# Block products for the last three token pairs of the first two QKV column groups, with the router's columns riding on them

## The chip, the cores and the metric

One core of one Trainium2 chip runs the whole layer in one program. The metric is the device time of one execution in microseconds, the median of several; lower is better.

## The reference

```python
xn = layernorm(x)                                  # [2048, 512]
qkv = xn @ wqkv                                    # 32 heads of 16, split into q, k, v
logits = q . k at 8 positions back, step 2         # sliding window, dilation 2
A = softmax(logits * 16**-0.5) @ v  ->  @ wo
top2 of  x @ w_gate (8 experts);  gates = softmax of the two
B = sum over the two experts  gate * silu(x @ w1[e]) @ w2[e]      # F = 1792
out = x + A(xn) + B(xn)
```

Both halves get the normalised input. Results are float32.

## The kernel before

**Numbers.** Matmuls take float16. A float32 operand is split into a rounded high part and a float16 remainder, and a product is three passes: high by high, low by high, high by low. So a QKV tile (128 tokens, one of four column groups `cg` of 3 x 128 columns, four blocks `kb` of the inner dimension) is twelve matmuls: passes `h` and `l` in line 384, pass `w` in line 382 (`q_pass`).

**Front.** Tokens are in 16 tiles `j`. Each is loaded, normalised (`ln_bn` to `ln_nm`), split (`x_hi`, `x_lo`), stored for the experts (`x_store`) and turned so that the inner dimension lies on partitions (`x_turn`, a DMA transpose on SyncE's queue, task `tn_j`; the first four tiles by TensorE). Column groups 0 and 1 go tile by tile (`seq`, line 1109). The router's eight columns stand beside group 0's weights (`gate_part`, lines 290 to 296): 400 columns in passes `h` and `l`.

**Block products.** Groups 2 and 3 are done for pairs of token tiles `p_` with Strassen's scheme (Winograd's form): seven products `m1` to `m7` of half the inner dimension instead of eight, each six matmuls of 384 columns (`product`, line 482). They need sums of feature blocks on VectorE for four tiles at a time (`f_join` L440, `s_sums` L447 to L450, `s_hi` on ScalarE L461, `s_lo` L464) and sums of weight blocks (`w_sum` L419, `u_hi` L430, `u_lo` L433). Results are put together by `take`: ScalarE copies `x11`, `x12`, `x22`, `xu`, `x21` (L506), VectorE adds `y11`, `y12`, `y22` (L508, L500). Products `m1`, `m6`, `m7`, `m4` add up in one PSUM bank, and between them ScalarE copies the bank out: `m6` waits for `x11`, `m7` for `x12`, `m4` for `xu`.

**Router.** When the last tile's gate columns are out of PSUM (`q_gl`, L407), VectorE runs `r_top` (L536 to L567), TensorE counts (`r_count`, L571), VectorE runs `r_rank` (L579 to L616) and three steps `r_hot` (L632 to L638), TensorE makes the token lists (`r_list`, L645, 16 matmuls twice), VectorE casts them (L648). GpSimd then gathers tokens (L852), SyncE turns them (L859), and TensorE begins with the first expert's `up` (L923). GpSimd's first list of constants is `c_lists`; the attention mask is `c_mask` (L233).

**Order.** A planner (`Plan.solve`) lists tasks with engine, cost, dependencies and due times, and fixes for each engine one order; every engine, and SyncE's DMA queue, then works in that order and waits where an operand is late. Attention's VectorE work (L781 on) fills the rest up to the end.

Of the kernel before, what the change touches and what calls it, by code (L numbers as in the profile page):

```python
# [17 lines left out]
P = 128  # L18
S = 2048
# [30 lines left out]
NPAIR = 10  # L50
# [6 lines left out]
NP0 = 0  # L57
# [5 lines left out]
class Plan:  # L63
    def __init__(self):
        self.tasks = {}

    def add(self, name, eng, dur, fn, deps=(), prio=0.0, svc=0.0, early=0.0, begun=(), lead=None, post=0.6):
        assert name not in self.tasks, name
        self.tasks[name] = (eng, dur, fn, [d for d in deps if d is not None], prio, svc, early,
                            [d for d in begun if d is not None], lead, post)  # L70

    def solve(self, start):
# [74 lines left out]
        self.begin, self.end, self.order, self.late = begin, end, order, late  # L147
# [19 lines left out]
def layer_kernel(ctx: ExitStack, tc, x, wqkv, wo, wg, w1, w2, out):  # L167
# [11 lines left out]
    qd = dp.tile([NCH, 3, 16 + S, H2], F32, name="qd")  # L179
# [18 lines left out]
    low_e = cp.tile([P, E, E], F32, name="low_e")  # L198
# [15 lines left out]
    def c_lists():  # L214
# [15 lines left out]
        nc.gpsimd.iota(it, pattern=[[1, MAXT]], channel_multiplier=0, **io)  # L230

# [13 lines left out]
    glog = rtp.tile([P, NJ, 2 * E], F32, name="glog")  # L245
# [44 lines left out]
    def gate_part():  # L290
        if 0 not in wq:
            wq[0] = frp.tile([P, KB, 784], F16, name="wq_0", tag="wq")
# [3 lines left out]
        nc.gpsimd.tensor_tensor(t[:, :, 392:400], gs, t[:, :, 384:392], op=ALU.subtract)  # L296
# [6 lines left out]
    def ln_bn(j):  # L303
        st = fre.tile([P, 6], F32, name=f"bs_{j}", tag="bs")
        v.bn_stats(st, xt_(j))
        mv = fre.tile([P, 2], F32, name=f"mv_{j}", tag="mv", bufs=4)
        v.bn_aggr(mv, st)
        L[j] = dict(mv=mv)

    def ln_rs(j):  # L310
        rs = fre.tile([P, 1], F32, name=f"rs_{j}", tag="rs", bufs=4)
        if j < N32:
            nc.scalar.activation(rs, L[j]["mv"][:, 1:2], AF.Sqrt, bias=eps, scale=1.0)
        else:
# [1236 lines left out]
```

## Time and profile before

| | |
|---|---|
| median of 3 runs | 759.71 us (759.58 to 759.80) |
| the profiled execution | 759.23 us |
| its span, first to last instruction | 757.5 us |
| TensorE busy | 750.4 us, 99% |
| VectorE busy | 665.1 us, 88% |
| ScalarE busy | 400.3 us, 53% |
| GpSimd busy | 110.3 us, 15% |

Times within the profile count from the first instruction; the profiled execution is 1.73 us longer than its span and 0.48 us shorter than the median. A busy share is an average over stages; a wait in TensorE's order counts fully only if it ends last.

### The profile page before, as it was taken

The page shows a single profiled execution, that of the slowest core. Times are in us where ns is not written, and L with a number is a line of the kernel's source. Part 1 is how long each engine was busy: PE and PEld are TensorE (multiplying, and loading weights), DVE is VectorE, ACT ScalarE, POOL GpSimd, SP SyncE. Part 2 cuts the span into 40 slices and gives each one's busy share as a digit, 9 for nine tenths or more (in the row PEclk, how much of TensorE's full clock was granted, in tenths as well). Part 3 has the DMA queues.
Part 4 walks back from the last instruction along what each step waited for, and adds up shares of the span by engine and source line. Part 5 has one row for each costly group of instructions (what it writes and reads, how often), then busy time and mean ns, then how long its engine had stood idle before and what let it go on. Part 6 is the DMA issues. An engine that isn't in the chain of part 4 may idle for free.

```text
span 757.5 us, 12466 instructions
## 1 busy us (share of the span) xinstructions
PE 750.4 (99%) x4950; PEld 415.7 (55%) x4950; DVE 665.1 (88%) x632; ACT 400.3 (53%) x596; POOL 110.3 (15%) x107
## 2 busy tenths in 40 slices
PE   8999999999999999999999999999999999999997
PEld 5555665555555555555555555555555555555544
DVE  8897999999999899989999989999999899737365
ACT  6875356555467445754654564465447554753300
POOL 2010036040001300300040004002100000007271
PEclk9999999999999999999999999999999999999999
DMA  8999899685359547994683599457526943986485
GB/s 279 225 267 333 277 213 316 246 230 180 119 179 218 184 158 218 217 227 121 223 250 127 193 245 260 132 179 211 204 85 170 247 129 112 219 325 203 138 255 192
DMA packets 167378, 157.26 MB, mean 208 GB/s; under 512 B 81505, under 2 KB 135137, under 8 KB 167059
## 3 DMA queue, kind: packets, MB, share of 16 engines
q1 hardware_dynamic: 161571, 139.52, 64.4%
q0 software_dynamic: 5216, 16.88, 7.6%
q8 instruction: 40, 0.66, 0.4%
q14 instruction: 23, 0.19, 0.1%
q10 hardware_dynamic: 528, 0.02, 0.0%
HBM read 108.12 MB, written 29.56 MB: 182 GB/s over the span
## 4 chain that ended last, share of the span: by engine, by line
PE 98%; SPq 1%; DMA 1%; DVE 0%; issue 0%; ACT 0%
PE pu L924 13%; PE pu L923 13%; PE pu L925 13%; PE y L956 10%; PE y L955 10%; PE y L954 10%; PE pw L1093 5%; PE pq L384 5%; PE pm_a L492 4%; PE yt L965 3%; PE pq L382 3%; PE pm_d L492 2%; PE yt L966 2%; PE yt L974 2%; PE yt L972 2%; PE yt L973 2%
## 5 line engine op out<-in xcount | busy, mean ns | idle before, releaser
L924 PE MATMUL pu<-xgt,w 128*128 128x64 f16 (+8 forms) x616 | 184.7, 321 | 0.0
L923 PE MATMUL pu<-xgt,w 128*128 128x64 f16 (+8 forms) x616 | 184.5, 321 | 0.0
L925 PE MATMUL pu<-xgt,w 128*128 128x64 f16 (+8 forms) x616 | 180.4, 321 | 0.0
L931 ACT ACTIVATE hs<-pu 128x64 f32<-128x64 f32 (+8 forms) x154 | 69.8, 481 | 183.8 <-PE pu L925 182.6
L898 DVE SCALAR_TENSOR_TENSOR w<-s,w 128x2048 f16<-128x2048 f32 (+1 forms) x57 | 128.3, 2250 | 18.6 <-ACT w L889 18.3
L889 ACT ACTIVATE w<-s 128x2048 f16<-128x2048 f32 (+1 forms) x57 | 107.3, 1883 | 60.2 <-PE yt L966 28.2
L956 PE MATMUL y<-w,hh 128*128 128x512 f16 x336 | 127.5, 379 | 0.0
L954 PE MATMUL y<-w,hh 128*128 128x512 f16 x336 | 127.5, 379 | 0.0
L955 PE MATMUL y<-w,hh 128*128 128x512 f16 x336 | 127.5, 379 | 0.0
L852 POOL DMA_INDIRECT xg<-xr,lis x35 | 65.6, 1874 | 419.3 <-DMA xgt<-xg 359.5
L941 DVE SCALAR_TENSOR_TENSOR hh<-hs,hh 128x550 f16<-128x550 f32 (+7 forms) x112 | 76.7, 687 | 26.2 <-ACT hh L937 26.1
L925 PEld LDWEIGHTS <-w 128*128 128x128 f16 x616 | 58.9, 97 | 48.4
L923 PEld LDWEIGHTS <-w 128*128 128x128 f16 x616 | 59.3, 98 | 40.9
L924 PEld LDWEIGHTS <-w 128*128 128x128 f16 x616 | 59.0, 98 | 40.8
L937 ACT ACTIVATE hh<-hs 128x550 f16<-128x550 f32 (+7 forms) x112 | 70.5, 630 | 3.4
L808 DVE TENSOR_TENSOR pv<-vt,at 128x4096 f32<-128x4096 f32 x16 | 70.8, 4422 | 0.3
L781 DVE TENSOR_TENSOR pq<-kt,qt 128x4096 f32<-128x4096 f32 x16 | 70.7, 4421 | 0.2
L785 DVE TENSOR_REDUCE at<-pq 128x256 f32<-128x4096 f32 x16 | 70.6, 4414 | 0.0
L1076 POOL DMA_INDIRECT yg<-yd,yrow x32 | 36.0, 1125 | 173.9 <-DMA s<-in_B_w 145.9
L814 DVE TENSOR_TENSOR pv<-pv 128x2048 f32<-128x2048 f32 (+1 forms) x32 | 56.1, 1754 | 0.2
L956 PEld LDWEIGHTS <-hh 128*128 128x128 f16 x336 | 32.9, 98 | 39.6
L955 PEld LDWEIGHTS <-hh 128*128 128x128 f16 x336 | 32.9, 98 | 34.1
(207 smaller groups left out, 1019.4 us busy)
## 6 DMA issues: line engine op xcount, KB each, us to landing
s<-in_B_w SPq DMA_DIRECT2D x112, 512.0 KB
kt<-qd SPq DMA_DIRECT2D x8, 960.0 KB
vt<-qd SPq DMA_DIRECT2D x8, 960.0 KB
qd<-qe SPq DMA_DIRECT2D x8, 768.0 KB
qd<-qp SPq DMA_DIRECT2D x8, 768.0 KB
yd<-ys SPq DMA_DIRECT2D x24, 256.0 KB
xr<-xh SPq DMA_DIRECT2D x16, 256.0 KB
qt<-qd SPq DMA_DIRECT2D x8, 512.0 KB
```

What stands on the lines that cost most here:

```text
L781: v.tensor_tensor(A["pr"].rearrange("p (j w d) -> p j w d", w=WIN, d=H2), a_win(A["k", c], hf, False), qb.to_broadcast([P, 8, WIN, H2]), o ...
L785: v.tensor_reduce(A["at", c][:, 8 * hf:8 * hf + 8].rearrange("p j w h -> p (j w h)"), A["pr"].rearrange("p (n d) -> p n d", d=16), axis=AX ...
L808: v.tensor_tensor(A["pr"].rearrange("p (j w h d) -> p j w h d", w=WIN, h=NH, d=16), a_win(A["v", c], hf, True), ab.to_broadcast([P, 8, WIN ...
L889: nc.scalar.activation(w[:, 0, c_], stg[k][:, c_], AF.Copy, scale=SW)
L898: v.scalar_tensor_tensor(w[:, 1, c_], stg[k][:, c_], SW, w[:, 0, c_], op0=ALU.mult, op1=ALU.subtract)
L923: nc.tensor.matmul(ps, a_[:, 0, kb, fs], xh, start=kb == 0, stop=False)
L924: nc.tensor.matmul(ps, a_[:, 0, kb, fs], xl, start=False, stop=False)
L925: nc.tensor.matmul(ps, a_[:, 1, kb, fs], xh, start=False, stop=kb == KB - 1)
L941: v.scalar_tensor_tensor(hh[:, 1, c_], hsd[key, f][:, c_], SH, hh[:, 0, c_], op0=ALU.mult, op1=ALU.subtract)
L954: nc.tensor.matmul(y_, hi, b_[:, 0, :], start=st, stop=False)
L955: nc.tensor.matmul(y_, hi, b_[:, 1, :], start=False, stop=False)
L956: nc.tensor.matmul(y_, lo, b_[:, 0, :], start=False, stop=sp)
```

## The change

Groups 0 and 1 (`s_` = 0) now go tile by tile only for the first ten tiles (pairs 0 to 4), and by block products for pairs 5, 6 and 7. All eight pairs of groups 2 and 3 (`s_` = 1) stay block products, in the order 4, 5, 6, 7, 0, 1, 2, 3. There are eleven block instances `i_` (`INST`), and every task name ends in `i_`: `m4_2` is product `m4` of pair 7 of groups 0 and 1.

The router's columns are 392 wide in all three passes (before: 400 in two). On the block pairs they ride on `m1`, `m7`, `m2` and `m4`, and ScalarE takes them out of three banks (`take_gate`); the last to come is that of `m4_2`. New are four weight sums and four split units for groups 0 and 1. The feature blocks come in the order 2, 3, 0, 1. The loads of the weights of groups 2 and 3 come after the units of groups 0 and 1. QKV results are stored per token pair (16 stores) in another layout of the scratch. The router's code is shortened by a few VectorE instructions (two memsets, three copies, a comparison with two sums, a subtraction). Normalisation takes two tiles' square roots in one instruction. The mask is set up on GpSimd right after the constants. The last instance keeps its bank `a` in another PSUM buffer. The warm-up matmuls are 11 of 512 columns instead of 44 of 128.

The diff, cut:

```diff
-NPAIR = 10
-NP0 = 0
+NP1 = 5
+SECOND = (4, 5, 6, 7, 0, 1, 2, 3)
+INST = [(0, p_) for p_ in range(NP1, NS)] + [(1, p_) for p_ in SECOND]
+NA, NI = NS - NP1, len(INST)
+BO = list(dict.fromkeys(p_ // 2 for _, p_ in INST))
...
+        nc.gpsimd.tensor_copy(tok16, tokf)
+        nc.gpsimd.memset(scan, 0.0)
+        nc.gpsimd.memset(mask, 0.0)
...
     def warm_up(n):
         for _ in range(n):
-            for q_ in range(KB):
-                nc.tensor.matmul(pwarm[:, q_ * P:(q_ + 1) * P], warm[:, 0:P], warm[:, q_ * P:(q_ + 1) * P], start=True, stop=True)
+            nc.tensor.matmul(pwarm, warm[:, 0:P], warm, start=True, stop=True)
...
+    def right_of(s_, n, a, k):
+        if s_:
+            return unit[1, n][:, a, k]
+        if n[0] == "b":
+            kh, cg = int(n[1]) - 1, int(n[2]) - 1
+            return wq[cg][:, 2 * kh + k, 392 * a:392 * a + (384 if cg else 392)]
+        return unit[0, n][:, a, k, 0:392 if n in ("t3", "t4") else 384]
...
+    def take_gate(i_, m):
+        p_ = INST[i_][1]
+        dst, bank = dict(m1=(glog[:, 2 * p_, :], "a"), m2=(gadd[:, p_ - NP1, :], "c"), m4=(glog[:, 2 * p_ + 1, :], "a"))[m]
+        nc.scalar.activation(dst, MB[i_, bank][:, 384:392], AF.Copy, scale=-1.0 / (SW * SX))
...
     seq = [(0, 0), (0, 1), (1, 0), (1, 1)]
-    seq += [(cg, j) for j in range(2, NPAIR) for cg in (0, 1)]
-    seq += [(0, j) for j in range(NPAIR, NJ)] + [(1, j) for j in range(NPAIR, NJ)]
-    seq += [(cg, j) for j in range(2 * NP0) for cg in (2, 3)]
+    seq += [(cg, j) for j in range(2, 2 * NP1) for cg in (0, 1)]
...
-    add("zero", "DVE", 0.6, lambda: v.memset(mask, 0.0), deps=["nm_5"])
-    add("c_mask", "POOL", 1.8, c_mask, deps=["zero"])
+    add("c_mask", "POOL", 1.8, c_mask, deps=["c_lists"])
...
-        add(f"lwq{cg + 2}", "SP", 2.6, B(load_wq, cg + 2, range(KB), nc.sync), deps=[f"wl{cg}_{kb}" for kb in range(KB)],
-            svc=2.7, begun=["tn_8"])
+        add(f"lwq{cg + 2}", "SP", 2.6, B(load_wq, cg + 2, range(KB), nc.sync), deps=[f"wl{cg}_{kb}" for kb in range(KB)] +
+            ([["ul0_t3", "ul0_t4"], ["ul0_t1", "ul0_t2", "t3_0", "t4_0"]][cg] if NA else []), svc=2.7, begun=["tn_8"])
...
         after = dict(m1=[], m2=[], m6=["x11"], m7=["x12"], m5=[], m4=["xu"], m3=["x22"])
+        if s_ == 0:
+            after["m7"] = ["x12", "gm1"]
...
-    gl = [f"gl_{j}" for j in range(NJ)]
-    add("r_top", "DVE", 6.2, r_top, deps=gl + ["c_lists"], prio=-10.0)
+    gl = [f"gl_{j}" for j in range(2 * NP1)] + [f"g{m}_{i}" for i in range(NA) for m in ("m1", "m2", "m4")]
+    add("r_top", "DVE", 5.3, r_top, deps=gl + ["c_lists"], prio=-10.0)
```

Three places show how instructions move.

**VectorE before the first results are added.** Before, the second feature block (`f_1`) and the weight sums stand ahead of the router's first row (L536), and no result of a block product is due yet:

```order
L440 TENSOR_TENSOR f_1_819<-xnT_103 128x2048
L447 TENSOR_TENSOR f_1_819<-f_1_819 128x4x128
L448 TENSOR_TENSOR f_1_819<-f_1_819 128x4x128
L449 TENSOR_TENSOR f_1_819<-f_1_819 128x4x128
L450 TENSOR_TENSOR f_1_819<-f_1_819 128x4x128
L419 TENSOR_TENSOR wqs_3_624<-wqs_3_624,wqs_2_778 128x768
L419 TENSOR_TENSOR wqs_3_624<-wqs_3_624 128x768
L433 SCALAR_TENSOR_TENSOR wx_b11_860<-wqs_2_778,wx_b11_860 128x768
L433 SCALAR_TENSOR_TENSOR wx_t1_895<-wqs_3_624,wx_t1_895 128x768
L419 TENSOR_TENSOR wqs_2_778<-wqs_3_624,wqs_2_778 128x768
L464 TENSOR_TENSOR sw_1_878<-f_1_819,sw_1_878 128x2x512 x2
L536 TENSOR_TENSOR lg_973<-glog_104 128x128
```

Now (`qp_0_5` is the output tile of pair 5, the first instance; `pm_0_c` its bank `c`):

```order
L495 TENSOR_TENSOR sw_2_760<-f_2_702,sw_2_760 128x2x512 x2
L462 SCALAR_TENSOR_TENSOR u0_t4_721<-wqs_0_160,u0_t4_721 128x2x384
L471 TENSOR_TENSOR f_3_804<-xnT_104 128x2048
L478 TENSOR_TENSOR f_3_804<-f_3_804 128x4x128
L479 TENSOR_TENSOR f_3_804<-f_3_804 128x4x128
L480 TENSOR_TENSOR f_3_804<-f_3_804 128x4x128
L481 TENSOR_TENSOR f_3_804<-f_3_804 128x4x128
L545 TENSOR_TENSOR qp_0_5_780<-qp_0_5_780 128x6x64
L554 SCALAR_TENSOR_TENSOR qp_0_5_780<-pm_0_d_797,qp_0_5_780 128x6x64
L554 SCALAR_TENSOR_TENSOR qp_0_5_780<-pm_0_c_762,qp_0_5_780 128x6x64
L495 TENSOR_TENSOR sw_3_850<-f_3_804,sw_3_850 128x2x512 x2
```

The second block's join and sums now stand ahead of the three sums of the first instance; the last of these, `y11_0`, frees the bank that TensorE's product `m2_2` writes.

**TensorE around the router's count.** Before, the count (`pr`) stands between the last tile of group 1 and the first block product:

```order
L382 MATMUL pq_1_15_1053<-wq_1_268,xnT_103 128x384
L571 LDWEIGHTS tri_73
L571 MATMUL pr_1068<-rsum_1006,tri_73 128x8
L572 LDWEIGHTS tri_73
L572 MATMUL pr_1068<-rsum_1006,tri_73 128x8
L492 LDWEIGHTS xnT_103
L492 MATMUL pm_0_a_1071<-wx_b11_860,xnT_103 128x384
```

Now it stands between two products of the fifth instance (pair 5 of groups 2 and 3), `m1_4` and `m6_4`, which share bank `a`:

```order
L531 MATMUL pm_4_a_1074<-wx_b11_899,xnT_104 128x384
L619 LDWEIGHTS tri_73
L619 MATMUL pr_1084<-rsum_1051,tri_73 128x8
L620 LDWEIGHTS tri_73
L620 MATMUL pr_1084<-rsum_1051,tri_73 128x8
L531 LDWEIGHTS sw_2_760
L531 MATMUL pm_4_a_1074<-wq_3_967,sw_2_760 128x384
```

`m1_5` and `m6_5` stand side by side in the same way. From the end of `m4_2`, whose gate columns come last, to the second half of the lists, TensorE's order holds 20 products and the first half of the lists.

**GpSimd at the start.** Before, the gate columns (L294 to L296) follow the constants, and the mask comes after them:

```order
L230 IOTA it_84 128x48
L294 TENSOR_SCALAR wq_0_211<-gs_186 128x4x8
L295 TENSOR_SCALAR gs_186<-gs_186 128x32
L296 TENSOR_TENSOR wq_0_211<-gs_186,wq_0_211 128x4x8
L233 AFFINE_SELECT mask_85<-mask_85 128x512
```

Now:

```order
L252 IOTA it_85 128x48
L253 CAST tok16_81<-tokf_77 128x16
L254 MEMSET scan_82 128x576
L255 MEMSET mask_86 128x512
L258 AFFINE_SELECT mask_86<-mask_86 128x512
L319 TENSOR_SCALAR wq_0_190<-gs_162 128x4x8
L320 TENSOR_SCALAR gs_162<-gs_162 128x32
L321 TENSOR_TENSOR wq_0_190<-gs_162,wq_0_190 128x4x8
```

The gate columns, which the first QKV matmul reads, moved behind two memsets and the mask.

## Rows read from the trace of the kernel before

**Rows 1.** The page of the profile, part 1: busy us, share of the span and instructions of each engine.
```profile
PE 750.4 (99%) x4950; PEld 415.7 (55%) x4950; DVE 665.1 (88%) x632; ACT 400.3 (53%) x596; POOL 110.3 (15%) x107
```

**Rows 2.** The chain of work that ended last, its shares of the span by engine (page, part 4).
```profile
PE 98%; SPq 1%; DMA 1%; DVE 0%; issue 0%; ACT 0%
```

**Rows 3.** Busy time by stretch of the span: stretch and its length, then busy us (and instructions) of PE, PEld, DVE, ACT, POOL, then granted clock, DMA share, GB/s.
```profile
20.00:30.00 10.00, 10.00 (x63) 5.89 (x62) 9.39 (x21) 9.38 (x24) 0.00 (x0) 1.00 0.95 196
...
50.00:60.00 10.00, 10.00 (x63) 5.90 (x62) 9.52 (x11) 6.29 (x13) 0.00 (x0) 1.00 1.12 244
60.00:70.00 10.00, 10.00 (x63) 5.95 (x62) 6.19 (x20) 4.60 (x11) 0.00 (x0) 1.00 1.04 359
...
90.00:100.00 10.00, 10.00 (x86) 6.25 (x83) 9.90 (x15) 5.29 (x10) 2.12 (x2) 1.00 0.80 249
```

**Rows 4.** The chain that ended last in order of time, 0 to 170 us: start, us, what. L384 and L382 are the passes of an ordinary QKV tile, L492 a block product.
```profile
48.55 1.35 PE pq L384 x8
...
70.32 1.30 PE pq L384 x8
...
88.90 0.98 PE pm_d L492 x6
...
90.27 0.98 PE pm_a L492 x6
```

**Rows 5.** ScalarE in order of time: start, us, engine, line, what, and in brackets the idle time before it and what ended it.
```profile
47.17 1.05 ACT L461 CAST sw<-f 128x1024 f16<-128x1024 f32 x1
50.59 1.25 ACT L402 ACTIVATE qe<-pq 128x384 f32<-128x384 f32 x3 [2.37 <-DMA qd<-qe]
...
64.89 0.18 ACT L407 ACTIVATE glog<-pq 128x16 f32<-128x16 f32 x1
```

**Rows 6.** VectorE in order of time around the second of its feature blocks (L440 joins, L447 to L450 sum, L464 splits).
```profile
49.51 2.29 DVE L440 TENSOR_TENSOR f<-xnT 128x2048 f32<-128x2048 f16 x1
51.84 0.69 DVE L447 TENSOR_TENSOR f<-f 128x512 f32<-128x512 f32 x1
...
59.49 2.35 DVE L464 TENSOR_TENSOR sw<-f,sw 128x1024 f16<-128x1024 f32 x2
```

**Rows 7.** VectorE in order of time, the router from its first row (L536) to the lists (L648); L500 is a sum of block products, L433 a unit of the product weights.
```profile
65.11 0.29 DVE L536 TENSOR_TENSOR lg<-glog 128x128 f32<-128x128 f32 x1 [3.26 <-ACT glog L407]
...
70.96 0.17 DVE L567 CAST rsum<-sc_a 128x8 f16<-128x8 f32 x1
...
75.05 0.16 DVE L579 COPY cnt<-pr 128x8 f32<-128x8 f32 x1
...
80.53 0.95 DVE L433 SCALAR_TENSOR_TENSOR wq<-wqs,wq 128x768 f16<-128x768 f32 x1
81.40 0.55 DVE L500 TENSOR_TENSOR qp<-qp 128x384 f32<-128x384 f32 x1
81.87 1.49 DVE L632 TENSOR_TENSOR oh<-io,col 128x1280 f16<-128x1280 f16 x1
...
85.73 2.28 DVE L638 TENSOR_TENSOR oh<-io,wh 128x2048 f16<-128x2048 f16 x1
...
90.60 2.29 DVE L638 TENSOR_TENSOR oh<-io,wh 128x2048 f16<-128x2048 f16 x1
...
96.51 0.19 DVE L648 CAST lis<-pl 128x40 int32<-128x40 f32 x1
```

**Rows 8.** SyncE, DMA issues in order of time: start, us of issuing, line, kind, what.
```profile
46.06 0.53 SPq L411 DMA_DIRECT2D qd<-qe  x1
46.64 3.48 SPq L273 DMA_DIRECT2D wqs<-in_A_wqkv  x4
50.22 6.81 SPq L347 DMA_TRANSPOSE xnT<-xh  x4
...
115.10 2.38 SPq L859 DMA_TRANSPOSE xgt<-xg  x1
```

**Rows 9.** GpSimd in order of time: start, us, line, what.
```profile
3.20 0.15 POOL L223 MEMSET low_e<- 128x64 f32 x1
...
4.61 0.30 POOL L294 TENSOR_SCALAR wq<-gs 128x32 f16<-128x32 f32 x1
...
41.67 2.54 POOL L233 TENSOR_SCALAR_AFFINE_SELECT mask<-mask 128x512 f32<-128x512 f32 x1 [36.06 <-DVE mask L1133]
...
127.80 1.84 POOL L987 MEMSET plane<- 128x1024 uint16 x2 [2.81 <-PE pm_a L492]
```

**Rows 10.** VectorE at the time of the third of these, and its usual L340 just before.
```profile
39.31 0.74 DVE L340 SCALAR_TENSOR_TENSOR xh<-xn,rs,xh 128x512 f16<-128x512 f32 x1
...
41.51 1.16 DVE L464 TENSOR_TENSOR sw<-f,sw 128x1024 f16<-128x1024 f32 x1
42.58 2.01 DVE L340 SCALAR_TENSOR_TENSOR xh<-xn,rs,xh 128x512 f16<-128x512 f32 x1
```

**Rows 11.** TensorE in order of time, at the start and at the first `up` matmul (L923).
```profile
7.46 0.51 PE L384 MATMUL pq<-wq,xnT 128*128 128x400 f16 x2 [0.15 <-ACT xnT L361]
...
12.55 0.63 PE L352 MATMUL pt<-ident,xn 128*128 128x128 f32 x4 [0.18 <-DVE xn L328]
...
127.57 0.37 PE L923 MATMUL pu<-xgt,w 128*128 128x486 f16 x1
```

More of the change, by code (lines that the diff above doesn't have):

```diff
@@ L70, in add @@
                             [d for d in begun if d is not None], lead, post)
+        self.behind[name] = list(behind)
     def solve(self, start):
@@ L146, in solve @@
         assert len(order) == len(tk), [n for n in tk if n not in begin][:20]
-        self.begin, self.end, self.order, self.late = begin, end, order, late
+        self.begin, self.end, self.late = begin, end, late
+        need, outs, prev = {n: 0 for n in tk}, {n: [] for n in tk}, {}
+        rank = {n: i for i, n in enumerate(order)}
+        for n in order:
+            e = tk[n][0]
+            for d in set(tk[n][3]) | set(tk[n][7]) | set(self.behind[n]) | ({prev[e]} if e in prev and e != "X" else set()):
+                outs[d].append(n)
+                need[n] += 1
+            prev[e] = n
+        heap = [rank[n] for n in tk if not need[n]]
+        heapq.heapify(heap)
+        self.order = []
+        while heap:
+            n = order[heapq.heappop(heap)]
+            self.order.append(n)
+            for o in outs[n]:
+                need[o] -= 1
+                if not need[o]:
+                    heapq.heappush(heap, rank[o])
+        assert len(self.order) == len(tk)
     def emit(self, names):
@@ L432, in u_lo, with pair_tile @@
-    def u_lo(n):
-        v.scalar_tensor_tensor(unit[n][:, 1], source[n](), SW, unit[n][:, 0], op0=ALU.mult, op1=ALU.subtract)
+                at_ = 392 if w_ == "w" else 0
+                nc.tensor.matmul(ps[:, 0:n], xs, wq[cg][:, kb, at_:at_ + n], start=w_ == "h" and kb == 0,
+                                 stop=w_ == "w" and kb == KB - 1, **kw)
+    EP, unit = {}, {}
+    def pair_tile(s_, p_):
+        if (s_, p_) not in EP:
+            EP[s_, p_] = frp.tile([P, 2, 3, 2, 2, H2], F32, name=f"qp_{s_}_{p_}", tag="qe", bufs=3)
+        return EP[s_, p_]
@@ L1249, in layer_kernel @@
         after = dict(m1=[], m2=[], m6=["x11"], m7=["x12"], m5=[], m4=["xu"], m3=["x22"])
+        if s_ == 0:
+            after["m7"] = ["x12", "gm1"]
         for i, (m, (bank, l_, r_)) in enumerate(prods.items()):
-            ready = [f"sl_{b}_{kb}" for kb in range(2)] if l_[0] == "s" else []
-            add(own(m), "PE", mm(*[384] * 6), B(product, p_, m), deps=[f"ul_{r_}"] + ready + [own(n) for n in after[m]] +
-                (free[bank] if m in ("m1", "m2", "m5") else []), prio=10.0 * len(seq) + 5.0 * (7 * (p_ - NP0) + i))
@@ new lines, in layer_kernel @@
+            add(own(m), "PE", mm(*[n] * 6), B(product, i_, m), deps=ready + [own(n) for n in after[m]] +
+                (free[bank] if m in ("m1", "m2", "m5") else []), prio=10.0 * len(seq) + 5.0 * (7 * i_ + i))
+            if n == 392 and m != "m7":
+                add(own("g" + m), "ACT", 0.22, B(take_gate, i_, m), deps=[own(m)])
+        keep = [stores[NP1 + i_ - 3]]
+        for n, m, more in (("x11", "m1", []), ("x22", "m5", []), ("x12", "m6", []), ("y12", "m3", ["x12"]), ("xu", "m7", []),
+                           ("y22", "m7", ["xu", "x22"]), ("y11", "m2", ["x11"]), ("x21", "m4", ["y22"] if i_ < NI - 1 else [])):
+            add(own(n), "ACT" if n[0] == "x" else "DVE", act(384) if n[0] == "x" else d2(384), B(take, i_, n),
+                deps=[own(m)] + [own(x) for x in more] + keep + ([f"m1_{i_}"] if n == "xu" and i_ == NI - 1 else []))
```

358 lines of the change are left out of this document (182 added, 176 removed).

## The prediction

> **What bounds the kernel now.** First the page: TensorE is busy for 750.4 us of a span of 757.5, 99% [rows 1]. Then the chain of waits: 98% of it is TensorE [rows 2]. Then the busy time by stretch: the four stretches of ten shown, from 20 us on, have TensorE at 10.00 and a granted clock of 1.00, while VectorE stands at 9.4 to 9.9 in three of them and at 6.19 in one [rows 3]. So TensorE's order runs without a gap, each matmul taken out is worth its time, and each new wait in that order costs its length. VectorE has little room in the first 130 us, and its order is fixed too. The reader is to see that the gain is certain and small, and that what decides is whether VectorE, ScalarE and the DMA queue keep ahead of TensorE in a front whose order is new.
>
> **What is removed.** A pair of tiles in groups 0 and 1 was 48 matmuls and is now 42, for three pairs 18 fewer. A product of six takes 0.98 us [rows 4], 0.163 us each: 18 x 0.163 = 2.9 us. Columns: before, 128 matmuls had 16 extra ones; now 192 have 8, so 512 column steps fewer. Eight of 400 columns take 1.35 us and eight of 384 take 1.30 [rows 4], 0.4 ns a column: 0.2 us. **Gain 3.1 us.** The warm-up has as many columns as before.
>
> **First new wait: the bank of the third instance.** TensorE reaches the end of the tenth tile at 48.4 us: its eleventh began at 48.55 [rows 4], less 0.1 for the columns. Up to `m2_2` stand nine products, five of them 392 wide, 8.9 us: it would be there at 57.3. `m2_2` writes the bank that `y11_0` frees. Two routes lead to `y11_0`, both through the join of feature block 3.
> By the engines: ScalarE copies out the tenth tile (0.4, as three in 1.25), then splits block 2 (first half 1.05 us) [rows 5], so 49.9. VectorE: two remainders (2.35 together, a half more for the wait on the second) [rows 6], a unit 0.9 (0.95 in rows), the join 2.3, four sums of 0.7, three sums of results at 0.47 each, 81.40 to 81.87 [rows 6, 7]: 49.9 + 2.4 + 0.9 + 2.3 + 2.8 + 1.4 = 59.7, and 0.2 until TensorE starts: 59.9, a wait of 2.6 us.
> By the DMA queue: the join needs the last transposes. Before, four of them were issued from 50.22 to 57.03, behind a weight load that took 3.48 us of the queue [rows 8]. That load is now behind them, so I take them as issued by 50.0. A store issued at 46.06 let ScalarE go on at 50.59 [rows 5, 8], 4.5 us later; the same for a transpose gives 54.5, and 54.5 + 2.3 + 2.8 + 1.4 + 0.2 = 61.2, a wait of 3.9. I take 3.2 between them, since nothing says which of the two comes last. Then `m5_1` waits for the remainders of block 3, which stand behind `y11_0` on VectorE (2.35 after it, against two products of 2.0 on TensorE): 0.3. **3.5 us, between 2.2** (VectorE 0.4 us sooner than its route above, and the 0.3 gone) **and 4.8** (the later route and 0.3, with 0.6 for a transpose that lands later than that store).
>
> **Second new wait: the router.** Before, the last gate columns were out at 64.89 + 0.18 [rows 5], the router began at 65.11, and its lists were cast at 96.51 [rows 7]. Now the same columns come with `m4_2`, and TensorE has 20 products (19.5 us) and one half of the lists, which is 0.4 (90.27 less 88.90 and one product) [rows 4]: 19.9 us. VectorE's chain there: out of PSUM 0.25; `r_top` was 65.11 to 71.13 [rows 7] and loses four instructions of about 0.1, 0.1, 0.2 and a part: 5.5; two sums 0.9; the count on TensorE and back 0.2; `r_rank` 75.05 to 80.53 [rows 7] less about 0.9 for what is cut: 4.6; one sum 0.5; the first list step two of 1.49, 2.9; two sums 0.9; the second 2.2 (2.28 in rows); a join 2.2; a sum 0.5; the third 2.3; 0.1 to TensorE (all by [rows 7]). Sum 23.0, so TensorE waits 3.1 us there, wherever in the stretch. Part of that does not depend on VectorE: `m1_4` and `m6_4` share a bank with nothing but the count between, as do `m1_5` and `m6_5`, and a copy out of PSUM is 0.42 us (1.25 for three [rows 5]), and I take 0.15 for a hand-over in either direction, above the 0.04 between the end of the gate copy and `r_top` [rows 5, 7], since a matmul has to drain: 0.7 twice. So **3.1, between 1.4** (those two alone) **and 3.6** (VectorE half a microsecond later). Behind the lists one product waits for a copy that waits for a sum: 0.3, between 0 and 0.5. The gathers and transposes of the first expert shift by as much as TensorE does; their last transpose was issued at 115.10 [rows 8], 12 us ahead of the first `up` at 127.57 [rows 11], so nothing is due there.
>
> **Start.** The gate columns, three instructions of 0.3, began at 4.61 [rows 9]; TensorE's first QKV matmul at 7.46 [rows 11] needs them. Now three of the constants before them are gone (a memset of 64 elements took 0.15 [rows 9]: 0.5 in all), but two memsets of some 0.5 each stand ahead (two of 1024 elements took 1.84 [rows 9]), and the mask. That took 2.54 at 41.67, while VectorE's sum from 41.51 held on for 1.16, and VectorE's next L340 took 2.01 instead of 0.74 [rows 9, 10]. With 1.5 to 2.5 for the mask the columns are ready at 4.6 - 0.5 + 1.0 + 1.5 + 0.9 = 7.5 to 8.5, up to 1.1 after that matmul's time; TensorE waited 0.18 at its next transposes, at 12.55 [rows 11], and wins that back. I take **0.4, between 0 and 1.3**: the upper end is what L340 lost, if a VectorE instruction of this start is held in the same way.
> The Trainium skill ("SBUF — State Buffer", Who interferes with whom) has a rule against this move: a VectorE instruction with two inputs in SBUF and a GpSimd one that reads SBUF share one read port, and whichever comes second is blocked for the whole of the other. The L340 row agrees with it. By the rule the mask would hold VectorE's weight remainders of that time, and the start would cost its upper end.
>
> **Costed at nothing.** The new weight sums and units (eight instructions of 0.95) stand on VectorE ahead of the chain above, in time that it had idle or gave to the first two joins. Stores per pair move the same bytes. If these covers are gone, block 2 is late and the first wait grows; that is in its upper end. Beyond the first expert's `up` TensorE's order is the same, so what is lost or won there stays.
>
> **Sum.** -3.1 + 3.5 + 3.1 + 0.3 + 0.4 = **+4.2 us**: 763.4 for an execution like the profiled one (759.23), and 763.9 beside the median of 759.71, which is 0.48 above it. Ends: -3.1 + 2.2 + 1.4 + 0 + 0 = +0.5 (760.2) and -3.1 + 4.8 + 3.6 + 0.5 + 1.3 = +7.1 (766.8).
>
> **Rivals.**
> *VectorE keeps ahead (faster).* One mechanism: the sums ahead of `y11_0` and the router's chain take less time than TensorE's work beside them, as in the kernel before, where the trace shows no wait for them. It decides at 19.9 us for the router's chain; from there only the adjacent products' 1.4 is left, and if ScalarE's and VectorE's latencies were hidden there too, the whole gain stands: 756.6. Against it: the chain sums to 23 us by rows of the same instructions, and its steps are back to back on VectorE. Chance 0.14.
> *Only the adjacent products wait.* The first wait is short because VectorE runs its front earlier, at 0.7 to 2.8 us, and the router's chain just fits: -3.1 + 0.7 + 1.4 + 0.4 = -0.6, to +1.5: 759.1 to 761.2, no change that a measurement can tell. For it: TensorE shows no wait in the stretch before, whatever VectorE had to do [rows 3]. Against it: the same 23 us. Chance 0.12.
> *The DMA queue is late.* It is full from 20 to 60 us (busy share 0.95 and 1.12 [rows 3]). If the transposes of pairs 6 and 7 land 2 us later than taken, TensorE waits ahead of the second instance already, and the weight loads of groups 2 and 3, which now start some 10 us later, hold ScalarE's copies: 2 to 4 us on top, 766 to 768. For it: the queue that a store waited 4.5 us in is the same. Against it: the weight load that stood ahead is gone. Chance 0.12; half of it lies in the range.
>
> **How the numbers follow.** Forecast (both waits, 760.2 to 766.8): 0.62, with the price of the sum. What a measurement of this kernel can tell from no change is about 0.2%, 1.5 us. Slower by more than that: 0.62 + 0.12 = 0.74; within: 0.12; faster: 0.14. The range goes from the second rival's lower end to the forecast's upper end, 759.1 to 766.8; it leaves out the faster case and the upper half of the DMA case, 0.14 + 0.06 = 0.20.
>
> **What would show it.** After: TensorE's waits in the first 130 us, absent before, of about 7 us in all; the longest, 1.7 to 3 us, ended by VectorE's result sum L554 near 60 us; waits of 0.6 to 0.8 us ended by ScalarE's copies (L552) near 81 and 89; one ended by VectorE's last list step (L681) near 97; the first `up` matmul near 131.5 instead of 127.57; and the same length from there to the end. I am wrong if the first `up` starts by 127.6, or if TensorE shows no gap between 50 and 105 us, or if the difference arises after it.

## The result, and the profile after

The changed kernel takes **767.18 us** (median of 4 runs, 766.39 to 768.51) beside 759.65 for the kernel before: ratio 1.0099, interval 1.0087 to 1.0111, so 7.5 us slower where the forecast said 4.2. The direction was right; the time lies 0.4 us above the upper end of the range, 766.8. In the profiled executions the span is 765.7 us where it was 757.5.

The page, part 1 (busy us, share, instructions) and the head of part 4, the chain that ended last:

```profile
PE 752.5 (98%) x4899; PEld 412.4 (54%) x4899; DVE 673.9 (88%) x633; ACT 402.5 (53%) x600; POOL 111.8 (15%) x110
...
PE 88%; DVE 7%; DMA 2%; ACT 1%; issue 1%; SPq 0%; DVEq 0%; ACTq 0%
```

It answers to [rows 1, 2]: TensorE has 51 instructions fewer and is busy 2.1 us longer, and the chain is TensorE for 88% where it was 98%, with 7% of VectorE in it. The stretches of ten, with the columns of [rows 3]:

```profile
50.00:60.00 10.00, 8.20 (x50) 4.50 (x48) 9.10 (x9) 4.73 (x11) 0.00 (x0) 1.00 1.02 251
60.00:70.00 10.00, 8.02 (x33) 3.84 (x32) 8.39 (x12) 5.88 (x12) 0.00 (x0) 0.66 1.07 305
...
80.00:90.00 10.00, 9.61 (x61) 5.69 (x59) 8.97 (x36) 2.95 (x6) 0.00 (x0) 1.00 0.25 80
90.00:100.00 10.00, 9.11 (x68) 5.27 (x66) 9.93 (x11) 2.86 (x6) 0.00 (x0) 1.00 0.87 279
100.00:110.00 10.00, 9.29 (x69) 5.50 (x69) 9.86 (x15) 5.50 (x10) 3.51 (x3) 1.00 0.98 334
110.00:120.00 10.00, 10.00 (x63) 6.01 (x62) 9.90 (x13) 5.70 (x11) 4.67 (x4) 1.00 1.09 295
```

Between 50 and 110 us TensorE stands still for 5.8 us in all (10 less its busy time, stretch by stretch; 70 to 80, not shown, has none), and in 60 to 70 a column that had been 1.00 throughout reads 0.66: the granted clock. So two things are lost there, time in which TensorE waits and time in which it works at the lower of its two levels. TensorE in order of time (start, us, form, in brackets the idle time before and what ended it; a line is one product or several):

```profile
49.24 1.16 PE L531 MATMUL pm_a<-wq,xnT 128*128 128x392 f16 x6
50.23 1.16 PE L531 MATMUL pm_c<-wq,xnT 128*128 128x392 f16 x6
51.69 1.17 PE L531 MATMUL pm_a<-wq,xnT 128*128 128x392 f16 x6 [0.30 <-DMA xnT<-xh]
...
56.61 1.16 PE L531 MATMUL pm_a<-u_t,sw 128*128 128x392 f16 x6
59.27 1.16 PE L531 MATMUL pm_a<-u_t,xnT 128*128 128x392 f16 x6 [1.50 <-ACT qp L552]
62.41 2.12 PE L531 MATMUL pm_c<-wq,xnT 128*128 128x392 f16 x6 [1.98 <-DVE qp L554]
64.32 2.16 PE L531 MATMUL pm_a<-wq,xnT 128*128 128x392 f16 x6
66.28 1.97 PE L531 MATMUL pm_d<-u_t,sw 128*128 128x384 f16 x6
68.09 1.14 PE L531 MATMUL pm_a<-u_t,sw 128*128 128x384 f16 x6
...
85.48 1.14 PE L531 MATMUL pm_a<-wq,sw 128*128 128x384 f16 x6 [0.34 <-ACT qp L552]
...
93.12 1.14 PE L531 MATMUL pm_a<-wq,sw 128*128 128x384 f16 x6 [0.58 <-ACT qp L552]
...
100.14 1.14 PE L531 MATMUL pm_a<-wx_b,xnT 128*128 128x384 f16 x6 [0.42 <-ACT qp L552]
101.82 0.57 PE L688 MATMUL pl<-oh 128*128 128x40 f16 x16 [0.55 <-DVE oh L681]
...
135.61 0.37 PE L966 MATMUL pu<-xgt,w 128*128 128x486 f16 x1
```

Each product should follow the one before by 0.975 us, or 0.995 with 392 columns. The row of 59.27 (`m4_0`) follows that of 56.61 by 2.66, so 1.67 were lost; the bracket shows 1.50, since the end of a product is modelled later than the start of the next. Read in this way:

| | forecast | measured | from |
|---|---|---|---|
| matmuls and columns saved | -3.1 | -3.1 (taken over, not measured apart) | |
| start | 0.4 | 0.95 | `m1_0` at 49.24; the eleventh tile of before at 48.39, less 0.1 for columns |
| waits of the first two instances | 3.5 | 4.28 | 0.47 at 51.69, 1.67 at 59.27, 2.14 at 62.41 |
| low clock | 0 | 2.7 | three products, 62.41 to 68.09, 5.68 instead of 2.97 |
| router and sums | 3.1 + 0.3 | 3.26 | 0.50, 0.74, 0.59 and 0.70 at the last rows but one, five of 0.06 to 0.21 |
| sum | +4.2 | +8.1 | first `up` at 135.61 where it was 127.57 [rows 11]: +8.04 |

The first `up` came 8.04 us later and the losses alone come to 11.19, so 3.15 is left for what was saved. The eleventh tile in the kernel before:

```profile
48.39 1.52 PE L384 MATMUL pq<-wq,xnT 128*128 128x400 f16 x8
```

From the first `up` to the end both executions take the same: 765.7 - 135.61 = 630.1, and 757.5 - 127.57 = 629.9.

What TensorE waited for at 59.27 and 62.41 stands in three rows: VectorE's join of feature block 3 and the last of the three sums (L554), and ScalarE's copies.

```profile
55.67 2.29 DVE L471 TENSOR_TENSOR f<-xnT 128x2048 f32<-128x2048 f16 x1 [0.79 <-DMA xnT<-xh]
...
61.72 0.55 DVE L554 SCALAR_TENSOR_TENSOR qp<-pm_c,qp 128x384 f32<-128x384 f32 x1
```

```profile
58.26 0.87 ACT L552 ACTIVATE qp<-pm_a 128x384 f32<-128x384 f32 x2 [1.93 <-DMA qd<-qp]
...
65.20 0.84 ACT L458 ACTIVATE wx_b<-wqs 128x768 f16<-128x768 f32 x1 [1.85 <-DMA wqs<-in_A_wqkv]
```

The join began at 55.67, when the last transposes had landed, 0.8 us after VectorE was free; `y11_0`, the sum of 61.72, ended at 62.27, and `m2_2` started 0.14 later. ScalarE's two copies at 58.26 waited for a store of SyncE's queue, and the second of them, `xu_0`, is what `m4_0` waited for. VectorE's rows from the join to `y11_0` follow each other without a gap, so `m2_2` would have started when it did without the wait at `m4_0` as well. The row of 65.20 shows ScalarE waiting 1.85 us for the weights of groups 2 and 3. At the start, GpSimd's mask and VectorE's first normalisation:

```profile
5.20 1.69 POOL L258 TENSOR_SCALAR_AFFINE_SELECT mask<-mask 128x512 f32<-128x512 f32 x1
...
8.05 0.35 POOL L321 TENSOR_TENSOR wq<-gs,wq 128x32 f16<-128x32 f32 x1
```

```profile
5.63 1.54 DVE L364 TENSOR_SCALAR xn<-x,mv,rs 128x512 f32<-128x512 f32 x1
...
7.28 0.55 DVE L364 TENSOR_SCALAR xn<-x,mv,rs 128x512 f32<-128x512 f32 x1
```

```profile
7.98 0.66 ACT L397 ACTIVATE xnT<-pt 128x256 f16<-128x256 f32 x2 [0.89 <-PE pt L388]
```

The normalisation (L364) of 5.63 took 1.54 us, the next one 0.55: it ended 0.28 us after the mask did. The first transposes came at 7.32 instead of 6.09, and ScalarE's first copy of them was done at 8.37. The gate columns (L321) were ready at 8.40. The first QKV matmul, which needs both, came at 8.42.

### The profile page after: what moved, and what is told of

Same layout as the page of the kernel before. It is cut to its first block, busy times and chain, and to the rows that moved or that the text cites. A ratio compares the mean times of both kernels' runs of the same rounds, so it can differ in the third digit from the quotient of the medians.

```text
span 765.7 us, 12383 instructions
## 1 busy us (share of the span) xinstructions
PE 752.5 (98%) x4899; PEld 412.4 (54%) x4899; DVE 673.9 (88%) x633; ACT 402.5 (53%) x600; POOL 111.8 (15%) x110
## 4 chain that ended last, share of the span: by engine, by line
PE 88%; DVE 7%; DMA 2%; ACT 1%; issue 1%; SPq 0%; DVEq 0%; ACTq 0%
PE pu L967 13%; PE pu L968 13%; PE pu L966 13%; PE y L997 9%; PE y L998 9%; PE y L999 9%; PE pw L1136 5%; PE yt L1008 3%; PE pm_a L531 3%; PE pm_d L531 2%; PE yt L1009 2%; PE yt L1016 2%; PE yt L1015 2%; PE yt L1017 2%; DVE bs L335 1%
## 6 DMA issues: line engine op xcount, KB each, us to landing
qd<-qp SPq DMA_DIRECT2D x16, 768.0 KB, 6.2
```

## The experiments

Times are medians; the kernel before ran beside each at 759.8 to 760.1. The times of the executions of one kernel, the changed one or a variant, lie 0.9 to 5.0 us apart, so next to each median stands where the first `up` came in the profiled execution, and, where the start differed, the time from `m1_0` to it (86.37 in the changed kernel).

| run | us | ratio, interval | first `up` | from `m1_0` |
|---|---|---|---|---|
| changed kernel | 767.18 | 1.0099, 1.0087 to 1.0111 | 135.61 | 86.37 |
| e1 mask late | 766.43 | 1.0090, 1.0076 to 1.0104 | 134.11 | 85.27 |
| e2 both waits filled | 769.76 | 1.0127, 1.0111 to 1.0142 | 135.25 | 86.02 |
| e3 first filled | 767.35 | 1.0102, 1.0087 to 1.0118 | 135.06 | 85.12 |
| e4 second filled | 766.77 | 1.0097, 1.0082 to 1.0113 | 134.78 | 84.45 |
| e5 no pair products | 760.56 | 1.0015, 1.0006 to 1.0024 | 128.53 | |
| e6 no weight loads | 767.18 | 1.0084, 1.0065 to 1.0102 | 136.61 | 86.43 |
| e7 no loads, both filled | 766.11 | 1.0094, 1.0071 to 1.0116 | 133.07 | 83.83 |
| e8 join later | 767.43 | 1.0095, 1.0079 to 1.0110 | 136.47 | 86.45 |
| e9 e5 with the mask moved | 761.18 | 1.0022, 1.0013 to 1.0031 | 128.89 | |
| e10 own bank | 767.07 | 1.0088, 1.0072 to 1.0103 | 134.89 | 84.93 |
| e11 one pair | 769.53 (one run) | | 137.87 | |
| e12 e5 with the mask last | 759.83 | 1.0000, 0.9991 to 1.0009 | 127.60 | |

**What the pair products cost (e5).** The theory against which the rest is measured: all waits but that of the start come from the pair products.

```diff
-NP1 = 5
+NP1 = 8
-    seq += [(cg, j) for j in range(2, 2 * NP1) for cg in (0, 1)]
+    seq += [(cg, j) for j in range(2, 10) for cg in (0, 1)]
+    seq += [(cg, j) for cg in (0, 1) for j in range(10, 2 * NP1)]
```

> All parts of the changed kernel but one: groups 0 and 1 go tile by tile for all sixteen tiles (the number of pairs that do is 8 instead of 5; from tile 10 on group 0 first, as in the kernel before); columns of 392, the shortened router, stores by pairs, the mask at the start and the rest stay. Theory: the block products of the first two groups bring all waits but that of the start and all of the fall of the clock; the first up matmul comes at 128.3 to 128.6 us (127.57, less 0.2 for the columns, plus 0.95 for the start) and the time is 760.4 to 760.8. Rival: the stores by pairs and the new layout hold the DMA queue or the tile buffers by themselves: 762 or more, with waits of TensorE between 40 and 70 us.

First `up` at 128.53, 760.56 us: as the theory said. After 14 us the trace shows no wait of TensorE above 0.14 us, and the granted clock stays at 1.00 between 48 and 80. So the pair products of three pairs, which save 2.9 us of matmuls, cost 6.6 us net (767.18 - 760.56).

**The start (e1, e9, e12).** In e1 the mask is moved alone:

```diff
+        nc.gpsimd.memset(mask, 0.0)          # into c_mask, out of c_lists
-    add("c_mask", "POOL", 1.8, c_mask, deps=["c_lists"])
+    add("c_mask", "POOL", 1.8, c_mask, deps=["c_lists", "gate", "swapR"])
```

> The changed kernel with the attention mask (its memset and its affine select) moved from ahead of the gate columns to behind them, after the first feature blocks' buffers are gone; nothing else. Theory: the mask's read at 5.20 to 6.89 us held VectorE's first normalisation (1.54 us instead of 0.55), so TensorE's front began 0.95 us late; with it gone every landmark up to 50 us comes 0.9 us sooner and the time is 766.2 to 766.4. Rival: the waits near 51 to 62 us hang on the DMA queue, which does not move with the start, and swallow the gain: 767.0 to 767.3, the waits there longer by 0.9.

766.43, just above what the theory gave (766.2 to 766.4), and an interval that overlaps that of the changed kernel: from the times alone nothing would follow. In the trace the first transposes came at 6.15 and `m1_0` 0.40 sooner, not 0.9 (the mask now ran at 43.5 us, behind GpSimd's copies of the gate columns into the units): a wait of 0.53 for ScalarE had come up at 40.94. The mask held VectorE in its new place too:

```profile
44.06 3.78 POOL L258 TENSOR_SCALAR_AFFINE_SELECT mask<-mask 128x512 f32<-128x512 f32 x1
```

```profile
46.32 1.90 DVE L478 TENSOR_TENSOR f<-f 128x512 f32<-128x512 f32 x1
...
48.25 0.69 DVE L479 TENSOR_TENSOR f<-f 128x512 f32<-128x512 f32 x1
```

The waits at 59 and 62 stayed (0.67 and 2.04 in the brackets), and one of 0.97 at 54.46 came in place of that at 51.69: 4.0 us in all instead of 4.3, so the rival, by which they would grow and swallow the gain, fell. `m2_2` came 0.48 us sooner, at 61.93. The first `up` came 1.50 us sooner; most of the rest is a low clock that lasted 3.4 us here instead of 6.8. So e1 does not show what the mask costs. The clean pair is e5 with the mask moved, tried twice:

> Both of the parts that cost time are undone: groups 0 and 1 tile by tile for all tiles, and the mask behind the gate columns; what is left of the change is the columns of 392, the shortened router, the stores by pairs and the order of the loads. Theory: the 0.7 to 0.9 us by which the kernel without the pair products was slower than before is the mask's hold on VectorE at the start, so this one is at 759.4 to 759.9, no different from before, and its first up matmul comes at 127.4 to 127.7 us. Rival: the stores by pairs or the later loads of the weights cost that, and it stays at 760.4 to 760.8.

It missed, with 761.18 instead of 759.4 to 759.9, because the edit did not do what its text said. Without pair products nothing else stands ahead of the mask on GpSimd, and it ran directly behind the gate columns. GpSimd's mask and VectorE's normalisations in e9:

```profile
5.63 0.52 POOL L257 MEMSET mask<- 128x512 f32 x1
6.22 1.75 POOL L258 TENSOR_SCALAR_AFFINE_SELECT mask<-mask 128x512 f32<-128x512 f32 x1
```

```profile
5.42 1.00 DVE L364 TENSOR_SCALAR xn<-x,mv,rs 128x512 f32<-128x512 f32 x1
...
6.53 1.72 DVE L364 TENSOR_SCALAR xn<-x,mv,rs 128x512 f32<-128x512 f32 x1
```

It held both normalisations now, 1.00 and 1.72 us instead of 0.55 each. In e12 the mask waits for the first gather (`deps=["ga0_0"]`) and runs at 105.74 us:

> As the kernel without pair products, with the mask (memset and affine select) after the first gather of GpSimd, near 110 us, where the previous attempt had it at 5.6 to 8.0 us, directly behind the gate columns, and held VectorE's two first normalisations there (1.00 and 1.72 us instead of 0.55). Theory: with the mask out of the first 13 us the start is that of the kernel before, the first transposes at 6.1 us, the first up matmul at 127.4 to 127.7 us and the time 759.4 to 760.0, no different from before. Rival: something else in what is left of the change costs the 0.7 us, and the time stays at 760.4 or more with the first up matmul after 128.2.

759.83, ratio 1.0000, first `up` at 127.60 where the kernel before has 127.57. With the pair products and the mask undone, what is left of the change (columns, router, stores, layout) costs and gives nothing that can be measured, and the mask is worth 0.93 us (128.53 - 127.60).

**The clock (e2, e3, e4).** Matmuls whose result nobody reads, in the waits:

```diff
     def product(i_, m):
...
+        for _ in range({(0, "m4"): 7, (2, "m2"): 9}.get((i_, m), 0)):   # e3: the first alone, e4: the second alone
+            nc.tensor.matmul(MB["f"], warm[:, 0:P], warm, start=True, stop=True)
```

> The changed kernel with 7 matmuls of 512 columns, whose result nobody reads, ahead of m4_0 and 9 ahead of m2_2 on TensorE, about as long as the two waits there (1.67 and 2.15 us of pitch). Theory: the granted clock fell to 0.50 at 61.4 us because TensorE had stood idle twice within 5 us; with the waits filled it stays at 1.00, the three products behind m2_2 take 2.98 us instead of 5.68, and the time is 764.3 to 764.8. Rival: the clock falls for another reason (the load of the chip as a whole), stays at 0.50 for six microseconds, and the time is 767 or, if the filling overruns the waits, 767.5.

> As with both filled, but only the first wait (7 matmuls ahead of m4_0). If the fall of the clock needs both waits, it stays at 1.00 and the time is about 764.5; if the second wait of 2.15 us alone brings it, the clock falls as in the changed kernel, at about 61.4 us, and the time is 767.2.

> As with both filled, but only the second wait (9 matmuls ahead of m2_2). If the second wait brings the fall, the clock stays at 1.00 and the time is about 764.5; if the first wait alone is enough, the clock falls some 3 us sooner than in the changed kernel, within the filling, and the time is 767 or more.

In the profiled executions the clock did what the theory said: with both or the second wait filled it stayed at 1.00 between 48 and 80 us; with the first alone filled it fell, at 63.6 us, behind the second wait. In the changed kernel it fell at 61.1, within that wait. Stretches of two in the changed kernel, in e3 and in e4 (columns as above):

```profile
60.00:62.00 2.00, 0.43 (x3) 0.04 (x1) 1.97 (x5) 1.10 (x2) 0.00 (x0) 0.78 0.92 201
62.00:64.00 2.00, 1.59 (x6) 0.73 (x7) 2.00 (x3) 1.35 (x3) 0.00 (x0) 0.50 1.13 319
64.00:66.00 2.00, 2.00 (x8) 0.92 (x7) 0.53 (x1) 0.80 (x2) 0.00 (x0) 0.50 1.18 289
66.00:68.00 2.00, 2.00 (x8) 0.96 (x7) 1.92 (x3) 1.40 (x5) 0.00 (x0) 0.51 1.09 332
```

```profile
62.00:64.00 2.00, 1.11 (x6) 0.67 (x7) 2.00 (x4) 1.82 (x4) 0.00 (x0) 0.91 1.07 308
64.00:66.00 2.00, 2.00 (x7) 0.91 (x6) 1.01 (x1) 0.48 (x1) 0.00 (x0) 0.50 1.14 305
66.00:68.00 2.00, 2.00 (x10) 1.05 (x9) 1.60 (x3) 1.95 (x6) 0.00 (x0) 0.74 1.11 321
```

```profile
62.00:64.00 2.00, 1.95 (x11) 0.90 (x10) 2.00 (x4) 1.78 (x4) 0.00 (x0) 1.00 1.11 314
64.00:66.00 2.00, 2.00 (x15) 1.20 (x13) 0.97 (x1) 0.14 (x1) 0.00 (x0) 1.00 1.12 292
66.00:68.00 2.00, 1.92 (x12) 1.05 (x11) 1.26 (x2) 1.91 (x5) 0.00 (x0) 1.00 1.13 321
```

So in these executions it is the second wait that brings the fall. How long TensorE then worked at 1.2 GHz was not the same: by this column the clock stayed at 0.50 for 6.8 us in the changed kernel and for 3.4 in e3, and so it did in e1 and e10. The products lost 2.7 us in the first and 1.6 to 1.8 in the other three; e3's shorter way from `m1_0` to the first `up`, 85.12, is mostly that. Nor did the fall come in every execution. The mean granted clock of the changed kernel's four is 0.992 to 0.997, but one of the four of e3, one of e6, one of e8 and two of e10 have 1.000.

But the time did not follow: 766.8 and 769.8 instead of 764.5. TensorE and ScalarE in e2:

```profile
66.57 1.14 PE L535 MATMUL pm_d<-u_t,sw 128*128 128x384 f16 x6
69.44 1.14 PE L535 MATMUL pm_d<-wq,sw 128*128 128x384 f16 x6 [1.73 <-ACT qp L556]
```

```profile
65.36 0.84 ACT L458 ACTIVATE wx_b<-wqs 128x768 f16<-128x768 f32 x1 [1.79 <-DMA wqs<-in_A_wqkv]
...
68.17 0.84 ACT L458 ACTIVATE wx_b<-wqs 128x768 f16<-128x768 f32 x1 [1.45 <-DMA wqs<-in_A_wqkv]
68.92 0.47 ACT L556 ACTIVATE qp<-pm_d 128x384 f32<-128x384 f32 x1
```

`m3_1`, at 69.44, lost 1.9 us waiting for the copy `x22_1` at 68.92, and that copy stood behind two splits of weights that waited for their loads, 1.79 and 1.45 us. At half the clock TensorE had not been early enough to notice. The clock stayed at 1.00 behind this wait. From `m1_0` to the first `up`, e2 gained 0.35, e4 1.9: there TensorE came to this place 1.1 us later, the second load was in, and `m3_1` waited 0.8. Why e2 then takes 633.0 us from the first `up` to the end, 2.9 more than the changed kernel, I did not settle: 1.4 of it is a wait of TensorE near 260 us, where ScalarE waited 5.2 us for a DMA, and the chain that ended last runs over gathers, VectorE's last sums and stores instead of TensorE.

**The loads of the weights (e6, e7).**

```diff
     def load_wq(cg, ks, eng):
+        if cg > 1:
+            wqs[cg] = wqs[cg - 2]
+            return
```

> The changed kernel without the loads of the weights of groups 2 and 3 (1.5 MB; their units are made from what the staging tiles of groups 0 and 1 hold, so the values are left out, not the work). Theory: these loads come late and hold ScalarE at 63.4 to 65.2 us and, once the clock is not low, again near 67, but with the clock at 0.50 TensorE is not waiting for ScalarE there: the first wait (52.3 to 62.4 us, the transposes) is unchanged, the clock falls as before, and the first up matmul moves by less than 0.5 us from 135.6. Rival: the late loads are the cause of the loss from 60 us on: it comes 2 us or more sooner.

> As without the loads of groups 2 and 3, and with both waits filled by 7 and 9 idle matmuls as in the run that filled both. There the clock stayed at 1.00 and TensorE then waited 1.9 us for ScalarE's copy x22_1. Theory: that wait came from the weight loads, so now the full price of the low clock comes out: the first up matmul at 132.9 to 133.5 instead of 135.6, 2.1 to 2.7 us sooner. Rival: VectorE, not the loads, sets the pace from 62 us on (its sums and units lie back to back), and it comes at 134.8 to 135.3 as with the loads.

In e6 the first `up` came at 136.61, 1.0 us later where the theory allowed 0.5; but `m1_0` was 0.9 late in this execution, and from there on it took 86.43, as before. Without the loads and with the waits filled, as the theory said, 133.07 and 83.83, 2.5 us sooner, nearly the whole price of the low clock. The two costs lie side by side: in the profiled executions, from `m1_0` to the first `up`, keeping the clock alone gave 0.35 us in e2 (1.9 in e4), and leaving out the loads alone nothing. (The median of e7, 766.11, moves by 1.1 only; its execution has a tail 1.2 us longer, 764.4 - 133.07.)

The times of single executions point the same way, though other things differ between them too. That of e6 without a fall (mean clock 1.000) took 764.44, the others, at 0.997, 0.995 and 0.992, took 766.80, 767.57 and 769.47. With the loads in place a missing fall gave less: 766.0 and 766.2 beside 767.9 and 768.0 in e10, 766.4 beside 766.9 to 768.1 in e8, and in e3 nothing, 767.1 beside 767.0 to 767.9.

**The bank and the order (e10, e8).**

```diff
-"c": (py, ("y0", "y2")[i_ % 2])
+"c": (py, "yt0" if i_ == 2 else ("y0", "y2")[i_ % 2])
```

> The changed kernel with another PSUM buffer (the one that the token lists use later) as bank c of the third instance, so that m2_2 no longer waits for y11_0; nothing else. Theory: m2_2 follows m4_0 without its wait of 2.15 us, but the next product, m1_2, needs bank a of the first instance, which ScalarE's copy frees after a sum that stands directly ahead of y11_0 on VectorE: it waits 0.7 to 1.2 us, and the rest is lost to ScalarE and the loads of the weights, as in the runs with filled waits; the first up matmul 0.5 to 1.5 us sooner, at 134.1 to 135.1. Rival: the bank alone is the cause of the first wait and of the fall of the clock, and the first up matmul comes at 131 to 132.

> The changed kernel with the join of the third feature block (2.2 us of VectorE between the second and the third list step) put behind the third list step, directly ahead of that block's sums. Theory: VectorE is full from 78 to 120 us (9.9 of 10), so the wait for the lists (0.70) and for m1_6 (0.58) goes, but the join's 2.2 us are missing later and come back as waits for copies and sums between 98 and 112 us: the first up matmul within 0.4 us of 135.6. Rival: the router's chain is what costs, as an order and not as a load: 1.0 to 1.3 us sooner, and 766.0.

In e10 the wait for the bank went, and `m1_2` waited 3.1 us instead:

```profile
59.59 1.16 PE L531 MATMUL pm_a<-u_t,xnT 128*128 128x392 f16 x6 [0.53 <-ACT gadd L559]
63.72 1.16 PE L531 MATMUL pm_a<-wq,xnT 128*128 128x392 f16 x6 [2.97 <-ACT glog L559]
```

The copy that it needs, `x21_0`, stood on ScalarE behind the split of block 3 (61.22 to 63.2). The clock fell all the same (0.50 at 66 to 68), but for 3.4 us. The first `up` came 0.7 us sooner, as expected, though the wait was longer than expected: from `m1_0` on e10 took 1.4 us less, 1.0 of it by the shorter low clock. From the first `up` to the end it took 1.3 us more. In e8 the waits at the lists and at `m1_6` went and came back as four of 0.35 to 0.55 us at 104 to 109. The first `up` came at 136.47, past the 0.4 us that the theory allowed; but `m1_0` was 0.8 late, and from there on nothing changed: 86.45. So this one other order won nothing: VectorE there is short of time, and the stretches of 90 to 120 above show it at 9.9 of 10.

**Fewer pairs (e11).** `NP1 = 7`.

> The changed kernel with one pair of tiles instead of three by block products in groups 0 and 1 (the number of pairs tile by tile is 7). It saves 6 matmuls, 1.0 us, instead of 18. Theory: the waits do not shrink with the pairs, since the router's columns still come with the last product of these groups and one instance has no second one between its products: the first up matmul at 133 to 137 us. Rival: waits in proportion to the pairs, a third of them: 130 to 131 us.

137.87, past the upper end of the theory. TensorE waits once for 4.9 us, for VectorE's `r_top`:

```profile
85.88 0.17 PE L619 MATMUL pr<-rsum,tri 128*128 128x8 f16 x1 [4.74 <-DVE rsum L615]
```

The clock fell at the end of it, to 0.50 for 3.4 us. One pair saves a third of the matmuls and costs more in this one wait than the three pairs at the router together (3.26): the theory's reason, that the router's columns come with the last product whatever the number of pairs, fits this row, but no run tested it by itself.

## Why the prediction was wrong

**The step that failed** is in its first part: "each new wait in that order costs its length". A wait of TensorE cost more than its length: after the second of them the granted clock was 0.50 for 6.8 us, and three products took 2.7 us longer. The working has no term for it, in the sum or at either end, although the profile of before gives the column in every stretch. The terms that it has, as measured, make -3.1 + 0.95 + 4.28 + 3.26 = +5.4, 765.1 beside the median and inside the range; with 2.7 at the upper end the range would have held 767.18. Taking the fall away would not have saved the forecast, though: with the waits filled the late weights held TensorE in its place, and the first `up` still came at 135.25 (e2). What the step left out is what stands behind a wait, here the low clock and, hidden by it, the weights.

**The gain**, 3.1: the trace leaves 3.15 for it, but no run measured it apart. e12 has the columns of 392 without the products, and its 0.2 us cannot be seen there.

**The first wait**, 3.5 between 2.2 and 4.8: 4.28, inside, but in part by luck. Of its two routes the DMA queue's was right, with 3.9 for `m2_2`: up to there the trace has 1.67 + 2.14 = 3.81, and the join waited for the transposes. The engines' route was 0.8 us shorter. That part of it would fall on `m4_0` was not seen, nor the cause, a store that SyncE issued behind four transposes. The other 0.47, ahead of the second instance, was not in the sum, and the 0.3 at `m5_1` did not come: the remainders were done at 64.5, and TensorE at the low clock came at 66.28.

**The router**, 3.1 and 0.3: 3.26. From the end of `m4_2` to the second list it was 22.9 us (78.9 to 101.82), where the chain had summed to 23.0. The waits came where it placed them, at `m6_4`, `m6_5` and the second list, at 0.50, 0.74 and 0.70. It took them for a chain; in e8 the same load came back as other waits, so it is VectorE's load in this stretch, which comes out the same in a sum and not in a remedy.

**The start**, 0.4 between 0 and 1.3: 0.95. The gate columns were ready at 8.40, inside the 7.5 to 8.5 of the forecast, and the first QKV matmul came at 8.42. That is near their late end, and the 0.18 us that TensorE was to win back at its next transposes [rows 11] it did not: it waited 0.17 there for VectorE, which was late as well. For the rule named there the text named the wrong victim: not the weight remainders but the first normalisation. Which of the two routes was the later in the changed kernel is open, 8.37 against 8.40; e9, where the gate columns were ready at 5.68 and the first QKV matmul came at 8.80, shows that the hold on VectorE alone is enough. The Trainium skill ("SBUF — State Buffer", Who interferes with whom) lists `tensor_scalar` in its two-port modes among what shares the pair with GpSimd, beside the two-input instructions that I had cited. The trace agrees: L364 is one, it took 1.54 us beside the mask in the changed kernel, and in e9 1.00 beside the memset and 1.72 beside the mask.

**The rivals.** That VectorE keeps ahead, and that only the adjacent products wait, fell. The late DMA queue was half right, and its 766 to 768 held the time: TensorE did wait for transposes ahead of the second instance, 0.47, and the weight loads did hold ScalarE's copies, but under the low clock, where they cost nothing more (e6). Its price came out only with the waits filled (1.9 at `m3_1` in e2).

**What would show it.** The waits were foretold as 7 us in all, and 7.5 were found; the first `up` near 131.5 (131.8 by the sum), and it came at 135.61, 0.6 of it by the start, 0.6 by the waits and 2.7 by the clock; the same length from there on, and it was.

## What to carry to other kernels

Where an engine is at 99%, a change that saves it work is worth that only if nothing behind it is later; take the neighbours' free time in the stretch first (here VectorE's, 0.1 to 0.6 us of ten in three of the four stretches of [rows 3]), and then the matmuls saved. A gap of TensorE is to be priced with what the clock does after it, and the column of the granted clock, with the pace of the matmuls beside it, says whether it did. And two losses that lie side by side hide each other: take them away together before you call either of them harmless.

## What the runs showed of the hardware

The granted clock also fell at the start of some executions. In e4 the warm-up ended at 5.54 and TensorE stood idle for 1.78 us until its first transposes; in the changed kernel it ended at 6.15, with 1.18 idle. Stretches of one in e4:

```profile
8.00:9.00 1.00, 1.00 (x6) 0.72 (x7) 1.00 (x3) 1.00 (x4) 0.35 (x1) 0.61 1.00 291
9.00:10.00 1.00, 1.00 (x5) 0.46 (x3) 1.00 (x4) 1.00 (x4) 0.00 (x0) 0.50 1.18 327
```

In e6 the gap was 2.17 us and the clock fell in the same way. In the changed kernel's profiled execution the same stretches read 1.00. The same eleven warm-up matmuls took 3.89 to 4.88 us in the executions profiled, so how much of the gap is left before the transposes differs from one execution to the next; with `m1_0` at 50.33 instead of 49.24 this was worth 1.1 us.

The column can miss a low clock at the start. In e8, e10 and e11 the first QKV matmuls followed each other by 0.33 us up to 10.4, the pace of the products at a granted clock of 0.50, where the changed kernel has 0.17, and `m1_0` came 0.7 to 0.8 late in e8 and e10, although the gap was 1.18 as in the changed kernel; the column still reads 1.00, as in this stretch of e8:

```profile
9.00:10.00 1.00, 1.00 (x5) 0.45 (x3) 0.87 (x3) 1.00 (x4) 0.00 (x0) 1.00 1.17 322
```

The changed kernel's four executions stand in the order of their mean granted clock: 766.39 at 0.997, 766.92 at 0.996, 767.45 at 0.995, 768.51 at 0.992. Falls at the start and longer or shorter falls at 61 us would both do that; how much each does was not tested. The clock need not be the whole of it: the kernel before, at 0.998 to 1.000, spreads by 1.0 to 2.1 us in its later groups of 9 to 15 runs.
